# Magnitude products in pieces of 1280 and 1600 for VectorE or GpSimd; argument casts all on VectorE

## The chip, the cores and the metric

The kernel runs on one core of one Trainium2 chip. The metric is the time of one execution on the device in microseconds (us), less is better. A core has five engines with their own instruction queues: TensorE (PE, matrix products; PEld is its weight load), VectorE (DVE), ScalarE (ACT), GpSimd (POOL) and SyncE (SP, which here only issues transfers). ScalarE and GpSimd queues can issue transfers too. Each queue is worked off in order; engines wait for each other by semaphores.

## The reference

With `x` of 2048 positions and 640 channels, the result is `g * a + (1 - g) * b`:

```python
g = sigmoid((x * gate_w).sum(-1))                       # a gate for each position
# a: a state space model, as a long convolution along the positions
P = exp((dt * A)[:, :, None] * l)                       # 640 channels, 128 states, l = 0..2047
K = einsum('dn,dnl,dn->dl', C, P, dt * B).real          # one filter of 2048 taps for each channel
a = irfft(rfft(x padded) * rfft(K padded))[:2048] + x * Dskip
# b: a gated MLP that mixes positions
z = gelu(x @ w_in);  z1, z2 = halves of z;  z2 = layernorm(z2)
b = (z1 * (w_sp @ z2 + b_sp)) @ w_out
```

`A`, `B` and `C` are complex, so each tap is a sum of terms "magnitude times sine or cosine": `exp(dt * Re(A) * l)` is the magnitude, and `dt * Im(A) * l` plus a phase is the argument of the sine.

## The kernel before

**The filter.** A position is split as `l = (rough part) + (fine part)`, and the filter comes out of small matrix products of two tables for each channel, with the 128 states on the partitions. The 640 channels are cut into eight chunks of 80 (`SD = 80`). For chunk `c`, `k_tables(c)` fills a tile `ET` with:

- `E1`: two halves (sine `E1s` and cosine `E1`) of `NA = 20` rows of 80, 1600 elements each;
- `E2` and `M2`: 33 rows each, the sine and the cosine of the other factor, of which rows 1 to 16 (`ps_`) and 17 to 32 (`ns_`) are 1280 elements each. The negative rows of `E2` are first copied with a changed sign.

There are two `ET` tiles, used in turn (`z = c % 2`), so chunk `c + 2` may write its tile only when chunk `c` has been read.

The steps of a chunk are:

1. `si`: the arguments, `th` times 8, 16, ... (an int32 tile of 8 rows of 80; the low 16 bits are the angle). VectorE does it as one product with a constant (L896); GpSimd did it as eight instructions, one a row (L258). There are two such tiles a chunk.
2. `ci`: the same plus a quarter turn (16384), for the cosine (L258).
3. `eights`: the arguments `ai` of `E1`, on VectorE (L856, L863), and their quarter-turn copies `ci2` (L258). Tiles `ia` (three) and `ib` (two) are rings.
4. ScalarE takes the sine of each tile (L312) and writes it to `ET`.
5. The products with the magnitudes `mr` (tables of exponentials): L912 on `E2`, L913 and L914 on the two halves of `M2`, L923 on both halves of `E1` at once. All were VectorE's.
6. TensorE's `ps_k` (`k_sub`, L940 and L941): 320 small matrix products for a chunk, which read the whole of `ET`.

The exponentials for four chunks at a time come from `k_exps` on ScalarE, ahead of chunks 0 and 4; they overwrite the `mr` that the four chunks before read.

**What surrounds it.** `ps_k` is evicted to `kf` and stored; after chunk 5 the first 480 channels are read back in another layout (`k_expand`, the `xk` loads), go through a first stage (`conv_s1`, L1029), and the second stage (`conv_s2`) multiplies with the transformed input: `ps_u` (L1076), `ps_s2k` (L1083), the product on VectorE (L1085), `ps_v` (L1091). Its twiddle tables T and G (`tg_build`) are built only when all eight `ps_k` are done, since they take the memory of the tables. The last stage is `conv_i2` (`ps_i`, L1157 and L1159, evictions L1107, L1124, L1126).

The MLP's work fills TensorE in between: `z2_tile` at the start (L486), `z1_tile` in groups (L518, with the groups 2 and 3 tied to the phases after chunks 1 and 5), and eight `sp_block`s (L704 and L706 for `ps_g`, evicted as `vT` by VectorE at L710 and L713; then L727 for `ps_o`). The forward transform of the input is `s1_u` (L545, L549).

**What sets the order.** No queue is written by hand. Every step is a task with a list of engines that may do it and a cost in us for each, what it reads and writes, and a bias. `Plan.run` goes through time with these costs and gives each engine, when it is free, the ready task of the highest priority; the tables' bias lets them go ahead of the MLP. The order found is then emitted, fixed, for all engines and for the transfers. So a change of a cost, or of the engines that a task may use, re-sorts every queue.

```python
    AE = ("DVE", "POOL")
    A1 = ("DVE",)
    dv2 = lambda n: 0.15 + n / 1920.0
```

Of the kernel before, what the change touches and what calls it, by code (L numbers as in the profile page):

```python
# [10 lines left out]
ALU = mybir.AluOpType  # L11
# [9 lines left out]
NA = len(ATAB)  # L21
# [15 lines left out]
class Plan:  # L37
# [15 lines left out]
    def add(self, eng, cost, fn, r=(), w=(), hold_=(), fset=None, nbytes=0, hold=0.0, bias=0.0, deps=(), lag=()):  # L53
        i = len(self.tasks)
        d = set(deps)
        d.update(j for j, _ in lag)
        hs = set(hold_)
        for k in r:
            if isinstance(k, tuple) and isinstance(k[0], Handle):
                hs.add(k[0])  # L60
            elif isinstance(k, Handle):
                hs.add(k)
            d.update(self.lastw.get(k, ()))
            self.readers.setdefault(k, []).append(i)
        for k in w:
            if isinstance(k, tuple) and isinstance(k[0], Handle):
                hs.add(k[0])
            elif isinstance(k, Handle):
                hs.add(k)
            d.update(self.lastw.get(k, ()))  # L70
            d.update(self.readers.get(k, ()))
            self.lastw[k] = [i]
            self.readers[k] = []
        d.discard(i)
        engs = (eng,) if isinstance(eng, str) else tuple(eng)
        costs = (cost,) if isinstance(cost, (int, float)) else tuple(cost)
        self.tasks.append(dict(i=i, engs=engs, costs=costs, fn=fn, deps=d, hs=hs, fset=fset, nb=nbytes, hold=hold, bias=bias, res=hold_, lag=dict(lag)))
        return i
# [139 lines left out]
def kernel(  # L218
# [20 lines left out]
    P = 128  # L239
# [11 lines left out]
    SD = 80  # L251
    DRAM = bass.MemoryType.DRAM
    PSUM = bass.MemoryType.PSUM
    vec, act, pool, pe, sp = nc.vector, nc.scalar, nc.gpsimd, nc.tensor, nc.sync

    def ts_(eng, out_, in_, s1, s2, op0, op1=None):
        if op1 is None:
            eng.tensor_scalar(out=out_, in0=in_, scalar1=s1, scalar2=None, op0=op0)  # L258
        else:
            eng.tensor_scalar(out=out_, in0=in_, scalar1=s1, scalar2=s2, op0=op0, op1=op1)  # L260
# [26 lines left out]
    add, ring = pl.add, pl.ring  # L287
    E_ = {"PE": pe, "DVE": vec, "ACT": act, "POOL": pool, "SP": sp}
# [4 lines left out]
    dv2 = lambda n: 0.15 + n / 1920.0  # L293
# [16 lines left out]
    def actf(cost, out_, in_, func, r, w, scale=1.0, bias=0.0, deps=(), lag=()):  # L310
        fs = {ACT.Exp: "exp", ACT.Tanh: "gelu", ACT.Ln: "exp", ACT.Sin: "sin", ACT.Arctan: "sin", ACT.Gelu_apprx_tanh: "gelu"}.get(func)
        return add("ACT", cost, lambda e: act.activation(out=out_(), in_=in_(), func=func, scale=scale), r=r, w=w, fset=fs, bias=bias, deps=deps, lag=lag)  # L312
# [54 lines left out]
    for g in range(4):  # L367
        S_(dma("SP", lambda g=g: xT[:, :, 512 * g:512 * g + 512], lambda g=g: x2[512 * g:512 * g + 512, :], 700000, w=[("xT", g)], tr=True,
              bias=7000 - g if g < 2 else 6800 - 10 * g))
# [72 lines left out]
    for q in range(4):  # L442
        add("DVE", 0.2, lambda e, q=q: ts_(vec, F1[:, q // 2, q % 2, :], f1b[:].rearrange("p c k -> p (c k)"), mqs[:, q:q + 1], None, ALU.mult),
            r=["pre"], w=[("F1", q)], bias=9000)
# [14 lines left out]
    th = parm.tile([P, D], F32, name="th")  # L459
# [99 lines left out]
    for g in range(4):  # L559
# [10 lines left out]
        for st in range(4 * g, 4 * g + 4):  # L570
            add(("ACT", "DVE"), (1.1, 0.5), lambda e, st=st: ts_(vec, z2n[:, st, :], z2n[:, st, :], mv[:, st, 0:1], rstd[:, st:st + 1], ALU.subtract, ALU.mult) if e == "DVE" else
                act.activation(out=z2n[:, st, :], in_=z2n[:, st, :], func=ACT.Identity, scale=rstd[:, st:st + 1], bias=nmr[:, st:st + 1]),
                r=[("nmr", g), ("rstd", g), ("z2", st)], w=[("z2n", st)], bias=8000)
# [54 lines left out]
    for o, a in (("ax", "Wr"), ("at", "Wi")):  # L628
        add("DVE", dv1(D), lambda e, o=o, a=a: vec.scalar_tensor_tensor(out=ap_(o), in0=ap_(a), scalar=-1.0, in1=ap_(a), op0=ALU.mult, op1=ALU.max),
            r=[a], w=[o], bias=2500)  # L630
# [9 lines left out]
    def pstt(o, a, s1, b, op0, op1):  # L640
        add("DVE", dv1(D), lambda e: vec.scalar_tensor_tensor(out=ap_(o), in0=ap_(a), scalar=s1, in1=ap_(b), op0=op0, op1=op1), r=[a, b, "ptmp"], w=[o], bias=2500)
# [24 lines left out]
    for ab in range(2):  # L666
        for q in range(2):
            add("DVE", 0.2, lambda e, ab=ab, q=q: vec.tensor_copy(out=f1p[:, ab, :].rearrange("p (c q k) -> p q c k", q=2, c=2)[:, q], in_=F1[:, ab, q, :].rearrange("p (c k) -> p c k", c=2)),
                r=F1r, w=[("f1p", ab, q)], bias=900)
# [149 lines left out]
    AE = ("DVE", "POOL")  # L819
    A1 = ("DVE",)  # L820
# [4 lines left out]
    def RI(tag, name, dt):  # L825
        return sbt(KGP, tag, name, shB, dt, bufs={"ia": 3, "ib": 2}[tag])
# [55 lines left out]
    def k_tables(c):  # L882
        B0 = KB0 - 50 * c
        z, zm = c % 2, c % 4
        sl = lambda t: t[:, SD * c:SD * c + SD]
        mr = lambda a, b: X["mr"][:, zm, a:b, :]
        E1, E2, M2 = (lambda: X["E1", z]), (lambda: X["E2", z]), (lambda: X["M2", z])
        add(("DVE", "ACT", "POOL"), (0.2, 0.27, 1.0), lambda e: act.copy(out=M2()[:, 0:1, :], in_=mr(0, 1)) if e == "ACT" else E_[e].tensor_copy(out=M2()[:, 0:1, :], in_=mr(0, 1)), r=[("mr", 0, zm)], w=[("M2z", z)], bias=B0)
        ids = []
        for g in range(2):  # L890
            si = RI("ia", "si", I32)
            ci = RI("ib", "ci", I32)

            def mk_si(e, si=si, g=g):
                if e == "DVE":
                    return vec.tensor_tensor(out=si()[:], in0=sl(th).unsqueeze(1).to_broadcast(shB), in1=cB[:, GB2 * g:GB2 * g + GB2].unsqueeze(2).to_broadcast(shB), op=ALU.mult)  # L896
                for j in range(GB2):
                    ts_(pool, row(si(), j), sl(th), 8.0 * (GB2 * g + j + 1), None, ALU.mult)
            add(AE, (0.95, 7.0), mk_si, r=["th", "kg"], w=[si], bias=B0)
            add(AE, (0.57, 2.6), lambda e, si=si, ci=ci: ts_(E_[e], ci()[:], si()[:], 16384.0, None, ALU.add), r=[si], w=[ci], bias=B0)  # L900
            gs = slice(GB2 * g + 1, GB2 * g + GB2 + 1)
            ids.append(actf(ac(GB2 * SD), lambda gs=gs: E2()[:, gs, :], lambda si=si: lo16(si()[:], shB), ACT.Sin, [si], [("E2p", z, g)], scale=SINS, bias=B0, deps=phase[0]))
            ids.append(actf(ac(GB2 * SD), lambda gs=gs: M2()[:, gs, :], lambda ci=ci: lo16(ci()[:], shB), ACT.Sin, [ci], [("M2p", z, g)], scale=SINS, bias=B0, deps=phase[0]))
        if c == 0:
            ids.append(add("ACT", 0.72, lambda e: act.activation(out=phi[:], in_=phi[:], func=ACT.Arctan), r=["phi"], w=["phi"], fset="sin", bias=B0 + 90, deps=phase[0]))
            pstt("phi", "phi", 8.0 * 65536.0 / (2.0 * PI), "al", ALU.mult, ALU.mult)
            ptt("phi", "phi", "be", ALU.add, ("DVE",))
        ep, mp = [("E2p", z, g) for g in range(2)], [("M2p", z, g) for g in range(2)]
        ps_, ns_ = slice(1, 17), slice(17, 33)
        mrp, mrn = [("mr", k, zm) for k in range(1, 17)], [("mr", k, zm) for k in range(17, 33)]  # L910
        add("DVE", dv4(16 * SD), lambda e: ts_(vec, E2()[:, ns_, :], E2()[:, ps_, :], -1.0, None, ALU.mult), r=ep, w=[("E2n", z)], bias=B0)
        add("DVE", dv2(32 * SD), lambda e: vec.tensor_tensor(out=E2()[:, 1:33, :], in0=E2()[:, 1:33, :], in1=mr(1, 33), op=ALU.mult), r=mrp + mrn + ep + [("E2n", z)], w=ep + [("E2n", z)], bias=B0)  # L912
        add("DVE", dv2(16 * SD), lambda e: vec.tensor_tensor(out=M2()[:, ns_, :], in0=M2()[:, ps_, :], in1=mr(17, 33), op=ALU.mult), r=mrn + mp, w=[("M2n", z)], bias=B0)  # L913
        add("DVE", dv2(16 * SD), lambda e: vec.tensor_tensor(out=M2()[:, ps_, :], in0=M2()[:, ps_, :], in1=mr(1, 17), op=ALU.mult), r=mrp + mp, w=mp, bias=B0)  # L914
        for gi, nr, ai in eights(lambda: sl(th), lambda: sl(phi), ["th", "phi", "kg"], B0):
            ci = RI("ib", "ci2", I32)
            sh = [P, nr, SD]
            add(AE, (dv2(nr * SD) + 0.09, 0.5 + nr * SD / 300), lambda e, ai=ai, ci=ci, nr=nr: ts_(E_[e], ci()[:, 0:nr, :], ai()[:, 0:nr, :], 16384.0, None, ALU.add), r=[(ai, j) for j in range(nr)], w=[ci], bias=B0)
            rs = slice(8 * gi, 8 * gi + nr)
            ids.append(actf(ac(nr * SD), lambda rs=rs: E1()[:, NA:2 * NA, :][:, rs, :], lambda ai=ai, nr=nr, sh=sh: lo16(ai()[:, 0:nr, :], sh), ACT.Sin, [(ai, j) for j in range(nr)], [("E1s", z, gi)], scale=-SINS, bias=B0, deps=phase[0]))  # L920
            ids.append(actf(ac(nr * SD), lambda rs=rs: E1()[:, 0:NA, :][:, rs, :], lambda ci=ci, nr=nr, sh=sh: lo16(ci()[:, 0:nr, :], sh), ACT.Sin, [ci], [("E1", z, gi)], scale=SINS, bias=B0, deps=phase[0]))
        ks = [(nm, z, q) for nm in ("E1", "E1s") for q in range(3)]
        add("DVE", dv2(2 * NA * SD), lambda e: vec.tensor_tensor(out=E1().rearrange("p (y a) d -> p y a d", y=2), in0=E1().rearrange("p (y a) d -> p y a d", y=2),  # L923
            in1=mr(33, 33 + NA).unsqueeze(1).to_broadcast([P, 2, NA, SD]), op=ALU.mult), r=[("mr", 33 + q, zm) for q in range(5)] + ks, w=ks, bias=B0)
        return ids

    SQ = 20
# [316 lines left out]
```

## Time and profile before

| | us |
|---|---|
| median of 3 runs | 402.55 (399.67 to 402.74) |
| the profiled execution | 403.62 |
| its span in the profile | 401.8 |
| TensorE busy | 330.6 (82% of the span) |
| VectorE busy | 280.2 (70%) |
| ScalarE busy | 240.2 (60%) |
| GpSimd busy | 155.8 (39%) |
| TensorE clock granted, mean | 0.939 of full speed |

A row of the groups has the line and the engine, the operation, what it writes and reads, the shape and the count; behind the first bar the busy time in us and the mean of one in ns; behind the second the idle time of the engine just before these instructions, with who ended it. A row of a timeline has the start in us, the time it took, the engine and the instruction; several alike in a row are merged ("x4" takes four), and the bracket tells how long the engine had been idle before, and for what. The slices cut the span into 40 parts; each digit is the busy share of an engine in tenths.

### The profile page before, as it was taken

To read this page: it belongs to the slowest core of one execution; us is meant where nothing else is said; L and a number is where in the kernel's file an instruction comes from. 1 tells how busy PE (TensorE), PEld (TensorE's weight loads), DVE (VectorE), ACT (ScalarE), POOL (GpSimd) and SP (SyncE) were. 2 spreads that over 40 slices of the span, in tenths; PEclk is the share of its full clock that TensorE was granted. 3 is DMA by queue.
4 is the path that set the end of the run, shared out by engine and by line. 5 is a ranking of instruction groups with operands and counts; after the bars stand their busy time and mean duration, and the time that the engine had idled before them with its cause. 6 is when DMAs were issued, how large, how long until landed. Compare 5 with 4: busy or idle time off the path is not lost. (4 is left out here: it accounts for less than half of the span.)

```text
span 401.8 us, 8388 instructions
## 1 busy us (share of the span) xinstructions
PE 330.6 (82%) x3218; PEld 213.9 (53%) x3225; DVE 280.2 (70%) x516; ACT 240.2 (60%) x425; POOL 155.8 (39%) x172
## 2 busy tenths in 40 slices
PE   0699589999999999999999955999978678863571
PEld 0255235667777667787776833776723233452220
DVE  4099981378988839784677757677588577999852
ACT  4187373299995667579924473555458657752240
POOL 3048840230077419672295639425475000000212
PEclk9999789999999999999999995999989989997586
DMA  7897729969883579393507249475435398530145
GB/s 174 161 168 116 164 63 183 295 152 239 192 207 100 131 174 255 106 184 44 139 0 124 69 67 229 131 239 124 146 105 172 98 298 285 150 89 2 33 137 165
DMA packets 111449, 59.37 MB, mean 148 GB/s; under 512 B 80262, under 2 KB 108050, under 8 KB 111410
## 3 DMA queue, kind: packets, MB, share of 16 engines
q1 hardware_dynamic: 109698, 55.02, 57.3%
q0 software_dynamic: 1712, 3.82, 3.5%
q8 instruction: 25, 0.41, 0.5%
q14 instruction: 14, 0.11, 0.1%
HBM read 24.73 MB, written 19.47 MB: 110 GB/s over the span
## 5 line engine op out<-in xcount | busy, mean ns | idle before, releaser
L704 PE MATMUL ps_g<-wT,z2n 128*128 128x256 bf16 (+1 forms) x896 | 113.3, 276 | 9.7 <-DVE vT L710 9.4
L704 PEld LDWEIGHTS <-z2n 128*128 128x128 bf16 (+1 forms) x896 | 87.3, 102 | 28.1 <-issue 9.8
L258 POOL TENSOR_SCALAR ci<-ai 128x640 int32<-128x640 int32 x11 | 29.3, 2673 | 65.9 <-ACT ET L312 41.1
L1085 DVE TENSOR_TENSOR p<-ps_s2k,us 128x960 bf16<-128x960 f32 (+1 forms) x48 | 47.9, 1038 | 8.5 <-PE ps_s2k L1083 6.6
L258 POOL TENSOR_SCALAR si<-th 128x80 int32<-128x80 f32 x64 | 43.7, 683 | 23.2 <-DVE t3p L653 18.1
L486 PE MATMUL ps_z<-Win,xT 128*128 128x432 bf16 (+1 forms) x160 | 35.2, 387 | 12.3 <-DMA xT<-in_A_u_dram 6.5
L1091 PE MATMUL ps_v<-p,G 128*128 128x480 bf16 (+1 forms) x128 | 26.2, 310 | 14.7 <-DVE p L1085 10.0
L1093 ACT CAST vs<-ps_v 128x480 bf16<-128x480 f32 (+1 forms) x48 | 24.7, 516 | 20.1 <-PE ps_v L1091 19.9
L312 ACT ACTIVATE ET<-ci 128x640 bf16<-128x640 int16 (+1 forms) x40 | 26.5, 676 | 13.2 <-DVE ci L258 9.2
L727 PE MATMUL ps_o<-Wout,vT 128*128 128x320 bf16 (+1 forms) x224 | 33.0, 299 | 0.0
L486 PEld LDWEIGHTS <-xT 128*128 128x128 bf16 x160 | 17.1, 107 | 29.9 <-issue 12.3
L518 PE MATMUL ps_z<-xg,Win 128*128 128x512 bf16 (+1 forms) x133 | 31.2, 379 | 0.6 <-ACT zt L312 0.2
L940 PE MATMUL ps_k<-ET 128*32 128x33 bf16 x640 | 27.7, 259 | 0.7 <-DVE ET L923 0.7
L319 ACT CAST us<-ps_u 128x480 bf16<-128x480 f32 (+1 forms) x48 | 24.7, 518 | 5.6 <-PE ps_u L1076 3.8
L940 PEld LDWEIGHTS <-ET 128*32 128x32 bf16 x640 | 26.8, 193 | 2.2 <-DVE ET L923 0.9
L1126 POOL TENSOR_TENSOR obr<-tm,obr 128x160 bf16<-128x160 bf16 (+1 forms) x8 | 4.9, 634 | 59.3 <-ACT tm L1124 53.5
L941 PE MATMUL ps_k<-ET 128*32 128x33 bf16 x640 | 27.6, 258 | 0.0
L1083 PE MATMUL ps_s2k<-fk,T 128*128 128x480 bf16 (+1 forms) x128 | 25.5, 312 | 2.0 <-DVE p L1085 1.6
L941 PEld LDWEIGHTS <-ET 128*32 128x32 bf16 x640 | 27.1, 195 | 0.0
L727 PEld LDWEIGHTS <-vT 128*128 128x128 bf16 (+1 forms) x224 | 21.5, 97 | 9.1
L490 ACT ACTIVATE z2n<-ps_z 128x864 bf16<-128x864 f32 x16 | 14.2, 885 | 19.9 <-PE ps_z L486 19.9
L1091 PEld LDWEIGHTS <-G 128*128 128x128 bf16 x128 | 10.2, 100 | 28.5 <-DVE p L1085 13.9
(188 smaller groups left out, 622.0 us busy)
## 6 DMA issues: line engine op xcount, KB each, us to landing
FU_d<-s1u SPq DMA_DIRECT2D x16, 240.0 KB
fu<-FU_d SPq DMA_DIRECT2D x16, 240.0 KB
fk<-FK_d SPq DMA_DIRECT2D x16, 240.0 KB
z_d<-zt SPq DMA_DIRECT2D x24, 128.0 KB
z1t<-z_d SPq DMA_DIRECT2D x8, 384.0 KB
xf<-in_A_u_dram SPq DMA_DIRECT2D x8, 320.0 KB
FK_d<-s1k POOLq DMA_DIRECT2D x5, 480.0 KB, 3.9
Win<-in_B_w_in_dram SPq DMA_DIRECT2D x2, 1080.0 KB
```

Of the source, the lines that this page charges most:

```text
L258: eng.tensor_scalar(out=out_, in0=in_, scalar1=s1, scalar2=None, op0=op0)
L312: return add("ACT", cost, lambda e: act.activation(out=out_(), in_=in_(), func=func, scale=scale), r=r, w=w, fset=fs, bias=bias, deps=deps ...
L319: (vec.tensor_copy if e == "DVE" else act.copy)(out=out_(), in_=in_())
L486: pe.matmul(ps()[:, h, 0:432 + h], lhsT=xT[:, i, 128 * st:128 * st + 128], rhs=Win2[:, i, 432 * h:432 * h + 432 + h], start=(i == 0), stop ...
L518: pe.matmul(ps()[0:fs, ft - f0, :], lhsT=Win1[:, i, 128 * ft:128 * ft + fs], rhs=xg()[:, i, :], start=(i == 0), stop=(i == ND - 1))
L704: pe.matmul(ps()[0:fs, ft - f0, :], lhsT=z2n[:, st, 128 * ft:128 * ft + fs], rhs=wT()[:, st, :], start=(st == 0), stop=False)
L727: pe.matmul(ps()[:], lhsT=vT[ft // 2]()[0:fs, ft % 2, 128 * r:128 * r + 128], rhs=Wout[0:fs, ft, HD * h:HD * h + HD], start=(ft == 0), sto ...
L940: pe.matmul(o_, lhsT=ET[:, 0:32, d], rhs=M2[:, :, d], start=True, stop=False, tile_position=(0, 32 * q))
L941: pe.matmul(o_, lhsT=ET[:, NA:NA + 32, d], rhs=E2[:, :, d], start=False, stop=True, tile_position=(0, 32 * q))
L1083: pe.matmul(ps()[:, i, W * n:W * n + W], lhsT=TK(k + n, i), rhs=fk()[:, j + n, :], start=True, stop=True)
L1085: add("DVE", dv1(2 * NW), lambda e, p12=p12, ps=ps, us=us: vec.tensor_tensor(out=p12()[:, :, 0:NW], in0=ps()[:, :, 0:NW], in1=us()[:, 0:NW ...
L1091: pe.matmul(pv()[:, W * n:W * n + W], lhsT=GV(k + n, i), rhs=p12()[:, i, W * n:W * n + W], start=(i == 0), stop=(i == 1))
```

## The change

- `si` and `ci` of `k_tables` may be done by VectorE alone; so may `ci2`. (GpSimd's eight-row form of `si` stays in the code, unused.)
- The product of 2560 elements on `E2` becomes two of 1280, one for the positive rows and one for the negative; the product of 3200 on `E1` becomes two of 1600, for `E1s` and `E1`. The two on `M2` keep their size.
- All six products of a chunk, 48 in all, may be done by VectorE or by GpSimd. The cost given for GpSimd is `0.45 + n / 700`, for VectorE `0.15 + n / 1920`.

```diff
-            add(AE, (0.95, 7.0), mk_si, r=["th", "kg"], w=[si], bias=B0)
-            add(AE, (0.57, 2.6), lambda e, si=si, ci=ci: ts_(E_[e], ci()[:], si()[:], 16384.0, None, ALU.add), r=[si], w=[ci], bias=B0)
+            add(A1, (0.95,), mk_si, r=["th", "kg"], w=[si], bias=B0)
+            add(A1, (0.57,), lambda e, si=si, ci=ci: ts_(E_[e], ci()[:], si()[:], 16384.0, None, ALU.add), r=[si], w=[ci], bias=B0)
...
-        add("DVE", dv2(32 * SD), lambda e: vec.tensor_tensor(out=E2()[:, 1:33, :], in0=E2()[:, 1:33, :], in1=mr(1, 33), op=ALU.mult), r=mrp + mrn + ep + [("E2n", z)], w=ep + [("E2n", z)], bias=B0)
-        add("DVE", dv2(16 * SD), lambda e: vec.tensor_tensor(out=M2()[:, ns_, :], in0=M2()[:, ps_, :], in1=mr(17, 33), op=ALU.mult), r=mrn + mp, w=[("M2n", z)], bias=B0)
-        add("DVE", dv2(16 * SD), lambda e: vec.tensor_tensor(out=M2()[:, ps_, :], in0=M2()[:, ps_, :], in1=mr(1, 17), op=ALU.mult), r=mrp + mp, w=mp, bias=B0)
+        PM = lambda n: (dv2(n), 0.45 + n / 700)
+        add(AE, PM(16 * SD), lambda e: E_[e].tensor_tensor(out=M2()[:, ns_, :], in0=M2()[:, ps_, :], in1=mr(17, 33), op=ALU.mult), r=mrn + mp, w=[("M2n", z)], bias=B0)
+        add(AE, PM(16 * SD), lambda e: E_[e].tensor_tensor(out=M2()[:, ps_, :], in0=M2()[:, ps_, :], in1=mr(1, 17), op=ALU.mult), r=mrp + mp, w=mp, bias=B0)
+        add(AE, PM(16 * SD), lambda e: E_[e].tensor_tensor(out=E2()[:, ps_, :], in0=E2()[:, ps_, :], in1=mr(1, 17), op=ALU.mult), r=mrp + ep + [("E2n", z)], w=ep, bias=B0)
+        add(AE, PM(16 * SD), lambda e: E_[e].tensor_tensor(out=E2()[:, ns_, :], in0=E2()[:, ns_, :], in1=mr(17, 33), op=ALU.mult), r=mrn + [("E2n", z)], w=[("E2n", z)], bias=B0)
...
-            add(AE, (dv2(nr * SD) + 0.09, 0.5 + nr * SD / 300), lambda e, ai=ai, ci=ci, nr=nr: ts_(E_[e], ci()[:, 0:nr, :], ai()[:, 0:nr, :], 16384.0, None, ALU.add), r=[(ai, j) for j in range(nr)], w=[ci], bias=B0)
+            add(A1, (dv2(nr * SD) + 0.09,), lambda e, ai=ai, ci=ci, nr=nr: ts_(E_[e], ci()[:, 0:nr, :], ai()[:, 0:nr, :], 16384.0, None, ALU.add), r=[(ai, j) for j in range(nr)], w=[ci], bias=B0)
...
-        ks = [(nm, z, q) for nm in ("E1", "E1s") for q in range(3)]
-        add("DVE", dv2(2 * NA * SD), lambda e: vec.tensor_tensor(out=E1().rearrange("p (y a) d -> p y a d", y=2), in0=E1().rearrange("p (y a) d -> p y a d", y=2),
-            in1=mr(33, 33 + NA).unsqueeze(1).to_broadcast([P, 2, NA, SD]), op=ALU.mult), r=[("mr", 33 + q, zm) for q in range(5)] + ks, w=ks, bias=B0)
+        for y, nm in enumerate(("E1s", "E1")):
+            ks = [(nm, z, q) for q in range(3)]
+            rs = slice(NA - NA * y, 2 * NA - NA * y)
+            add(AE, PM(NA * SD), lambda e, rs=rs: E_[e].tensor_tensor(out=E1()[:, rs, :], in0=E1()[:, rs, :], in1=mr(33, 33 + NA), op=ALU.mult), r=[("mr", 33 + q, zm) for q in range(5)] + ks, w=ks, bias=B0)
```

## The prediction

> **What bounds the kernel now.** I read the page's busy shares and slices first, to find the stage that the change touches.
>
> ```profile
> PE 330.6 (82%) x3218; PEld 213.9 (53%) x3225; DVE 280.2 (70%) x516; ACT 240.2 (60%) x425; POOL 155.8 (39%) x172
> ...
> PE   0699589999999999999999955999978678863571
> DVE  4099981378988839784677757677588577999852
> POOL 3048840230077419672295639425475000000212
> ```
>
> A slice is 10 us. From 60 to 270 us TensorE is busy nine tenths or more, but for slices 23 and 24; the change lies in 110 to 270, where the tables of the eight chunks are built. TensorE works there through a fixed order in which each chunk's `ps_k` (L940, L941) is placed just when its tables are due. The timelines of VectorE and TensorE:
>
> ```profile
> 119.75 1.83 DVE L923 TENSOR_TENSOR ET<-ET,mr 128x3200 bf16<-128x3200 bf16 x1 [1.15 <-ACT ET L312]
> ...
> 121.87 0.30 PE L940 MATMUL ps_k<-ET 128*32 128x33 bf16 x4
> ...
> 138.05 0.30 PE L940 MATMUL ps_k<-ET 128*32 128x33 bf16 x4 [0.72 <-DVE ET L923]
> ```
>
> Chunk 0's last product ends at 121.58 and its `ps_k` starts at 121.87; chunk 1 waits 0.72 us for it. A table later than planned is a stall. The one large stall:
>
> ```profile
> 243.31 0.83 DVE L896 TENSOR_TENSOR si<-th,cB 128x640 int32<-128x640 f32 x1 [1.70 <-POOL ci L258]
> ...
> 245.02 1.28 DVE L710 TENSOR_TENSOR vT<-ps_g,z1t 128x512 bf16<-128x512 f32 x2
> ...
> 245.76 3.57 PE L704 MATMUL ps_g<-wT,z2n 128*128 128x256 bf16 x16 [9.15 <-DVE vT L710]
> ```
>
> TensorE waits 9.15 us for an eviction that stands on VectorE behind an `si` that waits for GpSimd's cast. `ps_k` starts at 121.9, 138.1, 158.7, 176.8, 209.9, 227.5, 250.5 and 269.1; `ps_v`, the first output of the convolution's second stage, at 295.4, after which VectorE leads to the end (78.7 of 107 us busy). The groups by shape give the prices:
>
> ```profile
> L258 POOL TENSOR_SCALAR si<-th 128x80 int32<-128x80 f32 x64 | 43.7, 683 | 23.2 <-DVE t3p L653 18.1 <-ACT s1u L319 1.1
> L258 POOL TENSOR_SCALAR ci<-ai 128x640 int32<-128x640 int32 x11 | 29.3, 2673 | 65.9 <-ACT ET L312 41.1 <-DVE ai L863 23.9 <-ACT s1u L319 1.0
> L258 POOL TENSOR_SCALAR ci<-si 128x640 int32<-128x640 int32 x6 | 12.8, 2126 | 0.8 <-ACT ET L312 0.5
> L1126 POOL TENSOR_TENSOR obr<-tm,obr 128x160 bf16<-128x160 bf16 x6 | 2.8, 484 | 53.6 <-ACT tm L1124 53.5
> L1126 POOL TENSOR_TENSOR obr<-tm,obr 128x480 bf16<-128x480 bf16 x2 | 2.1, 1088 | 5.7 <-DMA obr<-ob_d 5.7
> L923 DVE TENSOR_TENSOR ET<-ET,mr 128x3200 bf16<-128x3200 bf16 x8 | 14.6, 1825 | 1.4 <-ACT ET L312 1.4
> L912 DVE TENSOR_TENSOR ET<-ET,mr 128x2560 bf16<-128x2560 bf16 x8 | 12.1, 1507 | 0.0
> L914 DVE TENSOR_TENSOR ET<-ET,mr 128x1280 bf16<-128x1280 bf16 x8 | 6.6, 828 | 0.0
> ```
>
> The number ahead of the second bar is the mean of one in ns. GpSimd's products exist only in two small shapes, in the tail.
>
> How a GpSimd product sits beside VectorE shows early in the timeline:
>
> ```profile
> 20.54 1.68 DVE L258 TENSOR_SCALAR mv<-zs 128x2 f32<-128x2 f32 x1 [0.57 <-ACT z2n L490]
> 20.77 1.41 POOL L600 TENSOR_TENSOR t<-nat_Cim,nat_Bim 128x640 f32<-128x640 bf16 x1
> ...
> 23.09 1.54 POOL L600 TENSOR_TENSOR Wr<-Wr,t 128x640 f32<-128x640 f32 x1 [0.91 <-DVE zs L565]
> 23.13 1.52 DVE L566 SCALAR_TENSOR_TENSOR mv<-zs 128x2 f32<-128x2 f32 x1
> ```
>
> Two-element VectorE instructions whose fellows take 0.15 us last until GpSimd's product ends.
>
> **What the Trainium skill says.** "SBUF — State Buffer", section "Who interferes with whom": VectorE's second port pair is GpSimd's only one; an instruction of VectorE with two SBUF inputs, or in a two-port mode, and a GpSimd instruction that reads SBUF exclude each other, whole instructions at a time. The trace agrees, with 1.5 and 1.4 us lost above. "GPSIMD Engine Reference", section 3.1: about 2.6 cycles an element at 1.2 GHz for two inputs, an estimate of 2.8 us for 1280; the trace's slope is smaller, (1088 − 484)/320 = 1.89 ns an element. "VectorE: DVE Perf Modes", the perf-mode tier table: bf16 products run two elements a cycle; the trace agrees (2560 in 1.507 us).
>
> **The change part by part.** By the queues of the changed kernel GpSimd takes 19 of the 32 products of 1280 and 7 of the 16 of 1600; VectorE keeps 13 and 9.
>
> *Products.* VectorE loses L912, L913, L914, L923: 12.1 + 6.6 + 6.6 + 14.6 = 39.9 us. It keeps 13 × 0.82 + 9 × 1.00 (between 828 for 1280 and 1507 for 2560) = 19.7. GpSimd: 1088 + 800 × 1.89 ns = 2.60 us for 1280 and 3.20 for 1600, so 19 × 2.60 + 7 × 3.20 = 71.8 us. Bounds: 2.28 and 2.74, the planner's own price (`PM`), from below; above, the stretch that GpSimd's casts show beside VectorE: `si` alone takes 0.416 us (median), `ci` 1.81, so 64 × 0.416 + 17 × 1.81 = 57.4 us became 85.8, 1.49 times.
>
> *Casts and arguments.* GpSimd loses these 85.8 us. VectorE gains 8 `si` at 0.825 = 6.6 (before.py's 64 pieces were 8 of them) and 17 `ci` at 0.505 = 8.6. Net: VectorE −5.0 us, GpSimd −14.0. Neither is worth that in time: both are sums over engines that are not full. What matters is that `si` was work ahead of need, and a product is the last step ahead of `ps_k`. No DMA is added or dropped, but the planner re-sorts the queues: GpSimd's stores of `kf` and its ten `xk` loads (0.55 us each) now stand between products of chunks 5, 6 and 7. The stall at 236 to 245 loses its cause.
>
> *The hold.* GpSimd's two-input work from 20.8 to 47 us (L600 7.1 us, L615 4.2) took from VectorE 1.5 + 1.35 + 0.45 + 0.54 + 0.64 + 1.4 = 5.9 us, read as each slow instruction less its fellows: 52%. At 71.8/8 = 9.0 us of products a chunk that is 4.7 us of VectorE's time a chunk. Queued behind a held instruction are the arguments of E1, the casts ScalarE's sines read, and `vT`, whose lateness stops TensorE. Bounds: nothing, if the holds fall into VectorE's idle time (VectorE is busy 90.2 of 128 us from 122 to 250), and all 4.7. I take a third, 1.6, plus the underpricing, 2 × 0.32 + 0.46 = 1.1: 2.7 us a chunk.
>
> *The order of TensorE.* I summed both orders at rates from the timeline's starts (L704 and L706 0.118 us each, L518 0.232, L727 0.137, L545 0.20, a `ps_k` 3.35). Between one `ps_k` and the next the old order holds 15.3, 20.6, 17.7, 31.8, 17.7, 11.4, 18.1; the trace has 16.2, 20.7, 18.0, 33.1, 17.6, 23.1, 18.6, so all but the 23.1 run without a stall. The new order holds 11.3, 19.1, 18.9, 19.5, 17.1, 14.6, 15.8, with 5.0 more before the first and 31.7 instead of 22.7 from the last `ps_k` to `ps_v`. It asks for tables sooner.
>
> The fourth gap can't be 19.5: from 174.9 ScalarE spends 19.8 us on exponentials, which overwrite what chunk 3's products read, then 1.3 on a table load and some 6.1 on sines, and then come the products, some 3.5: 31.
>
> *The sum.* First `ps_k` 121.9 + 5.0 + 2.7 = 129.6. Six gaps 96.8 + 6 × 2.7 = 113.0; the fourth 31; last `ps_k` 273.6. Plus 31.7: `ps_v` at 305.3, 9.9 later. The rest (106.4 us) I leave as it is: TensorE's order there is 2.3 us longer, beside VectorE. The profiled execution took 403.62 (span 401.8), the median is 1.07 less: 413.5 profiled, **412.5** as a median.
>
> **The rivals.** *Holds in idle time*: only the underpricing stays. 128.0, gaps 96.8 + 6.6 + 31, `ps_v` at 294.1: 401.3. For it speaks VectorE's idle share; against it, that VectorE is an in-order queue on the tables' path. *The shorter order comes true*: in addition chunk 3's products end early enough that the exponentials start ahead of `ps_k`, a fourth gap of 24: `ps_v` at 287.1, 8.3 earlier, 394. It decides where the last `ps_k` starts before 263.7 (295.4 − 31.7). For it speaks the old stall of 9.15 us that GpSimd's cast caused; against it, a product three times as long on GpSimd at the end of the chain. *Two thirds of the hold on the path*: 4.3 a chunk, `ps_v` at 316.5, 424. That the change does nothing is excluded: 26 products are in GpSimd's queue.
>
> **How the numbers follow.** One per cent, about what can be told from no change, is 4 us. Forecast (407 to 419) 0.54, the heavy hold 0.16, holds in idle time 0.17, the shorter order 0.13: slower 0.70, same 0.17, faster 0.13. The range of 396 to 425 leaves out most of the fastest case and the end of the slowest.
>
> **What would show it.** Right: GpSimd's 1280 products at 2.6 us or more; VectorE's short L856 and casts at several times their 0.2 and 0.5 us beside them; TensorE waiting at L940 for POOL; the last `ps_k` near 274. Wrong: VectorE's means unchanged, GpSimd's products near 2.3, or the fourth gap well below 31 with the last `ps_k` before 264.

## The result, and the profile after

The changed kernel takes 430.41 us (median of 4 runs, 428.94 to 433.97), the kernel before beside it 402.28: a ratio of 1.073, 95% interval 1.0645 to 1.081. It is slower by 28 us, where the forecast was 10 slower and the range ended at 425. The profiled execution took 433.97 us (span 432.1), before 403.62 (401.8). The page's busy shares and slices (a slice is now 10.8 us):

```profile
PE 342.6 (79%) x3220; PEld 218.5 (51%) x3225; DVE 323.8 (75%) x528; ACT 239.2 (55%) x424; POOL 156.6 (36%) x124
...
PE   0799599999777999578898998698999858865471
DVE  3189940898987949989469998984549767899852
POOL 2157810000743605581225829655267030000111
PEclk9999699999968969796888999899999999998586
```

VectorE was to lose 5 us of work and 37.6 us to the hold (4.7 in each of eight chunks), and is busy 43.6 us longer; TensorE does the same work in 12 us more. TensorE's row of nines, which before ran from slice 6 to slice 28 but for 23 and 24, is broken from slice 10 (108 us) on. How it starts, in the timelines of the three engines for chunk 0 (start, time taken, engine, instruction; in the bracket the idle time before and its releaser):

```profile
109.49 2.61 POOL L915 TENSOR_TENSOR ET<-ET,mr 128x1280 bf16<-128x1280 bf16 x1 [23.82 <-DVE ET L258]
109.78 2.99 DVE L600 TENSOR_TENSOR phi<-phi,be 128x640 f32<-128x640 f32 x1
113.44 5.80 DVE L856 SCALAR_TENSOR_TENSOR ai<-th,phi 128x80 int32<-128x80 f32 x6
113.59 2.69 POOL L914 TENSOR_TENSOR ET<-ET,mr 128x1280 bf16<-128x1280 bf16 x1 [1.50 <-DVE ET L913]
116.24 2.60 POOL L916 TENSOR_TENSOR ET<-ET,mr 128x1280 bf16<-128x1280 bf16 x1
120.34 0.54 DVE L258 TENSOR_SCALAR ob<-ps_o,omg 128x320 bf16<-128x320 f32 x1
120.94 2.03 PE L727 MATMUL ps_o<-Wout,vT 128*128 128x320 bf16 x7 [5.13 <-DVE ob L258]
122.76 5.21 PE L704 MATMUL ps_g<-wT,z2n 128*128 128x256 bf16 x28
128.36 3.22 POOL L927 TENSOR_TENSOR ET<-ET,mr 128x1600 bf16<-128x1600 bf16 x1 [0.76 <-ACT ET L312]
128.43 3.24 DVE L856 SCALAR_TENSOR_TENSOR ai<-th,phi 128x80 int32<-128x80 f32 x1
132.32 2.33 PE L704 MATMUL ps_g<-wT,z2n 128*128 128x256 bf16 x16 [3.39 <-DVE vT L710]
```

Six adds of 80 elements (L856) last 5.80 us, from 113.44 on, while GpSimd's two products run from 113.59 to 118.84; one add lasts 3.24 us, as long as the product of 1600 that began 0.07 us before it. Behind the six adds stands the eviction `ob` (L258). It takes its usual 0.54 us, but TensorE has waited 5.13 us for it, and its next 28 matmuls of L704 take 5.21 us. The groups by shape (busy time, mean ns of one):

```profile
L927 POOL TENSOR_TENSOR ET<-ET,mr 128x1600 bf16<-128x1600 bf16 x7 | 26.2, 3747 | 12.5 <-ACT ET L312 12.5
L856 DVE SCALAR_TENSOR_TENSOR ai<-th,phi 128x80 int32<-128x80 f32 x64 | 25.8, 447 | 2.0 <-ACT ET L312 2.0
L863 DVE SCALAR_TENSOR_TENSOR ai<-th,ai 128x160 int32<-128x160 f32 x16 | 14.3, 895 | 0.0
L258 DVE TENSOR_SCALAR ci<-ai 128x320 int32<-128x320 int32 x8 | 12.8, 1599 | 0.7 <-ACT ET L312 0.7
L914 POOL TENSOR_TENSOR ET<-ET,mr 128x1280 bf16<-128x1280 bf16 x4 | 10.5, 2620 | 1.7 <-DVE ET L913 1.5
L914 DVE TENSOR_TENSOR ET<-ET,mr 128x1280 bf16<-128x1280 bf16 x4 | 11.0, 2738 | 0.0
```

GpSimd's 1280 products take 2.6 to 2.8 us on the mean and its 26 products 78.2 us in all, near the 71.8 forecast. It is VectorE's rows that are off: an add 447 ns (279 before), the 160-wide one 895 (321), the 320-wide cast 1599 (345). The four L914 products that VectorE kept take 2.74 us each where GpSimd needs 2.62.

The eight `ps_k` start at 138.9, 151.0, 179.1, 207.3, 236.1, 253.4, 271.3 and 290.8, `ps_v` at 326.6; after that come 105.5 us (106.4 before). So all of the loss lies ahead of `ps_v`. TensorE's waits for evictions and tables (total us, times, longest):

```profile
PE ps_g L704 <- DVE vT L710: 8.3, 5, 3.4
PE ps_o L727 <- DVE ob L258: 5.8, 2, 5.1
PE ps_s1x L549 <- ACT s1u L319: 4.3, 1, 4.3
PE ps_k L943 <- DVE ET L927: 3.0, 2, 2.8
PE ps_k L943 <- POOL ET L927: 1.9, 1, 1.9
```

It waits more for VectorE's evictions (14.1 us) than for tables (6.5 with the 1.6 at L944); the 4.3 us are one wait for an eviction of ScalarE. All but the first line are new or grew. The wait for `vT` was 9.4 us before, nearly all of it the one stall of 9.2, which is gone; the five now are others.

### The profile page after: what moved, and what is told of

It reads as the page before. It is cut to its first block, busy times and chain, and to the rows that moved or that the text cites. A ratio compares the mean times of both kernels' runs of the same rounds, so it can differ in the third digit from the quotient of the medians.

```text
span 432.1 us, 8357 instructions
## 1 busy us (share of the span) xinstructions
PE 342.6 (79%) x3220; PEld 218.5 (51%) x3225; DVE 323.8 (75%) x528; ACT 239.2 (55%) x424; POOL 156.6 (36%) x124
## 5 line engine op out<-in xcount | busy, mean ns | idle before, releaser
L704 PE MATMUL ps_g<-wT,z2n 128*128 128x256 bf16 (+1 forms) x896 | 119.6, 285 | 9.7 <-DVE vT L710 8.3
L704 PEld LDWEIGHTS <-z2n 128*128 128x128 bf16 (+1 forms) x896 | 89.5, 105 | 37.1 <-issue 15.7
L727 PE MATMUL ps_o<-Wout,vT 128*128 128x320 bf16 (+1 forms) x224 | 38.4, 331 | 7.5 <-DVE ob L258 5.8
L312 ACT ACTIVATE ET<-ci 128x640 bf16<-128x640 int16 (+1 forms) x40 | 25.8, 678 | 25.5 <-DVE ci L258 25.5
L727 PEld LDWEIGHTS <-vT 128*128 128x128 bf16 (+1 forms) x224 | 23.7, 106 | 21.6 <-issue 10.2
L1094 PE MATMUL ps_v<-p,G 128*128 128x480 bf16 (+1 forms) x128 | 25.6, 306 | 10.8 <-DVE p L1088 9.5
L518 PE MATMUL ps_z<-xg,Win 128*128 128x512 bf16 (+1 forms) x135 | 32.6, 389 | 1.2 <-ACT zt L312 0.8
L913 POOL TENSOR_TENSOR ET<-ET,mr 128x1280 bf16<-128x1280 bf16 x7 | 19.4, 2765 | 32.0 <-ACT ET L312 24.7
L927 POOL TENSOR_TENSOR ET<-ET,mr 128x1600 bf16<-128x1600 bf16 x7 | 26.2, 3747 | 12.5 <-ACT ET L312 12.5
L944 PE MATMUL ps_k<-ET 128*32 128x33 bf16 x640 | 27.9, 258 | 2.1 <-DVE ET L916 1.6
L944 PEld LDWEIGHTS <-ET 128*32 128x32 bf16 x640 | 27.4, 195 | 0.0
L888 POOL COPY ET<-mr 128x80 bf16<-128x80 bf16 x6 | 4.9, 817 | 61.9 <-PE ps_k L944 32.7
L856 DVE SCALAR_TENSOR_TENSOR ai<-th,phi 128x80 int32<-128x80 f32 x64 | 25.8, 447 | 2.0 <-ACT ET L312 2.0
L1086 PE MATMUL ps_s2k<-fk,T 128*128 128x480 bf16 (+1 forms) x128 | 24.5, 299 | 1.2 <-DVE p L1088 0.7
```

The lines of the kernel that those rows point to most:

```text
L518: pe.matmul(ps()[0:fs, ft - f0, :], lhsT=Win1[:, i, 128 * ft:128 * ft + fs], rhs=xg()[:, i, :], start=(i == 0), stop=(i == ND - 1))
L704: pe.matmul(ps()[0:fs, ft - f0, :], lhsT=z2n[:, st, 128 * ft:128 * ft + fs], rhs=wT()[:, st, :], start=(st == 0), stop=False)
L727: pe.matmul(ps()[:], lhsT=vT[ft // 2]()[0:fs, ft % 2, 128 * r:128 * r + 128], rhs=Wout[0:fs, ft, HD * h:HD * h + HD], start=(ft == 0), sto ...
L856: add("DVE", 0.12 + dv1(SD), lambda e, j=j, r_=r_, t=t: vec.scalar_tensor_tensor(out=row(t(), j), in0=src(), scalar=float(ATAB[r_]), in1=a ...
L927: add(AE, PM(NA * SD), lambda e, rs=rs: E_[e].tensor_tensor(out=E1()[:, rs, :], in0=E1()[:, rs, :], in1=mr(33, 33 + NA), op=ALU.mult), r=[ ...
L944: pe.matmul(o_, lhsT=ET[:, NA:NA + 32, d], rhs=E2[:, :, d], start=False, stop=True, tile_position=(0, 32 * q))
```

## The experiments

The theories. A: GpSimd's product holds VectorE, whole instructions at a time; what queues behind the held ones, evictions and arguments, makes TensorE late. B: the delay alone: tables come late, since the planner prices GpSimd too low and the last steps ahead of `ps_k` take three times as long. C: the casts moved to VectorE, or the split, cost the time. D: the lower clock of TensorE is a cause of its own.

### The same plan, all products issued by VectorE

```diff
-add(AE, PM(16 * SD), lambda e: E_[e].tensor_tensor(...))
+add(AE, PM(16 * SD), lambda e: vec.tensor_tensor(...))
```

The same edit on all six products. The plan is made with the old prices and engines, so every queue but VectorE's and GpSimd's keeps its order.

> The plan and the order of every queue stay those of the changed kernel, but the 26 products that stood in GpSimd's queue are issued by VectorE. Theory A (GpSimd's two-input products hold VectorE): VectorE loses some 48.6 us of hold and gains 19 x 0.82 + 7 x 1.00 = 22.6 us of products, so its busy time falls from 323.8 to about 298, the mean of the argument adds (L856) from 447 to below 300 ns, and the time from 430 to 400-412. Theory B (the leaner order of TensorE and the moved casts cost the time, whichever engine multiplies): the time stays at 420-432. Theory D (TensorE's clock fell by itself): 420-430 with the granted clock in the table stage still near 0.86.

It took 400.7 us (median of 4 runs, 395.1 to 402.2). The ratio on record, 0.985 of before (0.977 to 0.993), rests on two of the four and is unclear. As it would have been a gain, it was run again:

> The same kernel as in the first set of runs (the changed kernel's plan, all products issued by VectorE), with more rounds, since it stood below the kernel before. Theory A with the order of TensorE worth what the sum said (8.3 us less up to ps_v where tables are in time): 395-400. If the first reading was chance: 400-404.

Here 400.27 us (22 runs), 0.9954 (0.993 to 0.998): half a per cent under before. It is the base for what follows. The groups, waits and `ps_k` stretch of this second profile:

```profile
L856 DVE SCALAR_TENSOR_TENSOR ai<-th,phi 128x80 int32<-128x80 f32 x64 | 12.1, 232 | 1.9 <-ACT ET L312 1.9
L863 DVE SCALAR_TENSOR_TENSOR ai<-th,ai 128x160 int32<-128x160 f32 x16 | 5.1, 317 | 0.0
L258 DVE TENSOR_SCALAR ci<-ai 128x320 int32<-128x320 int32 x8 | 2.5, 318 | 1.1 <-ACT ET L312 1.1
L914 DVE TENSOR_TENSOR ET<-ET,mr 128x1280 bf16<-128x1280 bf16 x8 | 6.5, 816 | 0.0
```
```profile
PE ps_g L704 <- DVE vT L710: 1.8, 5, 0.5
PE ps_o L727 <- DVE ob L258: 1.0, 2, 0.6
```

Every mean is back (add 232 ns, cast 318), and `ps_k` waits for nothing. VectorE is busy 286.3 us; without the 26 products (19 of 0.816 and 7 of 0.98, 22.4 us) that is 263.9, against 323.8 in the changed kernel: **59.9 us of hold**, 77% of the 78.2 us that GpSimd's products took. The clock, in the windows from 110 us to `ps_v` (columns: busy time of TensorE, its weight loads, VectorE, ScalarE and GpSimd, each with its count; granted clock; DMA share; GB/s), first of the changed kernel and then of this one:

```profile
110.00:326.63 216.63, 185.51 (x2301) 131.80 (x2303) 172.42 (x265) 113.56 (x182) 109.05 (x65) 0.90 0.48 115
```
```profile
110.00:293.09 183.09, 172.80 (x2317) 127.43 (x2320) 136.78 (x295) 116.36 (x186) 37.73 (x39) 0.99 0.60 138
```

With the products off GpSimd the clock is at 0.99 by itself, so D falls as a cause of its own. Of the 33.5 us between the two, 12.7 is TensorE's own work at a lower clock and 20.8 is idle. (At 110 us the changed kernel stood some 2.6 us further in the same order, so what its tables lost is a little more.) That the clock falls after stalls is what the Trainium skill says ("TensorE: Matmul & The Clock Gate", Part 1: the array is throttled unless it is busy); the trace agrees in the 28 matmuls of L704, 3.22 us in this kernel and 5.21 soon after the stall of 5.13. The leaner order of TensorE (this expectation's B) and C's casts are in this kernel too and cost nothing. The kernel takes hold and delay away together; further runs below part them.

### The products on VectorE with a plan made for it; the split alone; the products alone

```diff
-PM = lambda n: (dv2(n), 0.45 + n / 700)
-add(AE, PM(...), ...)
+PM1 = lambda n: (dv2(n),)
+add(A1, PM1(...), ...)
```

> The split products and the casts all on VectorE, and the plan made for that. Theory A: no hold is left, VectorE is busy 280.2 + 15.2 (casts) + about 2 (more and shorter products) = 297 us, and the time is 398-408. Theory C (the casts on VectorE or the split itself cost the time): 412-430, with VectorE late ahead of the ps_k of the tables.

406.12 us, 1.010 (1.0065 to 1.013): within the expectation of A, and about 1% over before.

The split alone has this edit, and takes `si`, `ci` and `ci2` back to `AE` with their old prices:

> Only the split: six products a chunk, all on VectorE, the casts and arguments for VectorE or GpSimd as before. Theory A: no new hold, two more fixed costs of VectorE a chunk (48 x 0.82 or so against 39.9 us in all, under 3 us): within 1.5% of before, 397-408. Theory C' (the split itself costs): over 410.

400.98 us, 0.9957 (0.993 to 0.998): the split costs nothing. The products alone keep the changed kernel's products and take the casts back to `AE`:

> Only the products are changed: split, for VectorE or GpSimd (this plan gives GpSimd 15 of 1280 and 1 of 1600, 42.2 us); the casts and arguments may go to GpSimd as before. Theory A: slow, by the hold of 42.2 us of products, 33.7 x 42.2 / 71.8 = 20 us over what the plan gives without: 412-425. Theory C (the loss comes from the casts on VectorE): within 1% of before, 398-407.

424.6 us, 1.055 (1.050 to 1.060), with the casts where they were before. A's 20 us are 23.6 over the split alone. C falls on both sides: the casts without products on GpSimd cost at most 1%, the products without the casts over 5%.

### The true price in the plan

```diff
-PM = lambda n: (dv2(n), 0.45 + n / 700)
+PM = lambda n: (dv2(n), 0.17 + n / 528)
```

> The changed kernel with GpSimd's price in the plan raised to what the trace measured (0.17 + n/528: 2.59 us for 1280, 3.20 for 1600, instead of 2.28 and 2.74). Theory B (the plan places ps_k too early since the price is too low): 405-415. Theory A: the holds remain as far as products remain on GpSimd; with 20 or more products there the time is 418-432.

441.6 us, 1.096 (1.090 to 1.1025), outside both expectations, and slower than A had it. The plan still gives GpSimd 25 products (19 of 1280, 6 of 1600) and VectorE is busy 329.0 us. B's part that speaks of the price falls; why this plan loses 11 us more than the changed kernel's isn't settled. The price that is missing is on the other engine: no figure for GpSimd's own time tells the planner that VectorE stands meanwhile.

### One input instead of two

```diff
+for s in (in0, out):
+    pool.tensor_scalar(out=out, in0=s, scalar1=1.0, scalar2=0.0, op0=ALU.mult, op1=ALU.add)
```

in place of each `tensor_tensor` of GpSimd.

> Each product in GpSimd's queue is replaced by two in-place multiply-by-one-and-add-zero instructions with one SBUF input, on the same tiles and in the same place in every queue. It leaves out those multiplications by the magnitudes. Theory A in its narrow form (the second input is what holds VectorE): VectorE's means go back (L856 below 320 ns, the 320-wide cast to about 0.35 us) and the time falls to 400-414, if the pair on GpSimd takes no longer than the 2.6 or 3.2 us of the product. Theory A in its broad form (any GpSimd instruction on SBUF holds VectorE): 420-435. Theory B (tables late because GpSimd's step is the last of the chain, with no hold needed): 420-432 with VectorE's means gone back.

422.99 us, 1.049 (1.043 to 1.055). The pair takes 3.06 us for 1280 instead of 2.6, and VectorE, busy 313.0 us, loses 49.1 of the pairs' 84.0 us, 58%. Its means don't go back as B had it: an add takes 338 ns, the 320-wide cast 968. So A holds in its broad form: that GpSimd reads SBUF with one input is enough to hold VectorE. Not all of the loss need be hold here, since the pair also comes later: TensorE waits 5.3 us for GpSimd at `ps_k`.

### The bench: who holds whom

A kernel of its own: five streams of VectorE, each alone and beside four streams of GpSimd that start with it.

```diff
+vec.tensor_copy(out=sv[:, 0:1], in_=sg[:, 1:2])
+pool.tensor_copy(out=sg[:, 0:1], in_=sv[:, 0:1])
+for _ in range(gc): gf(tg)
+for _ in range(cnt): vf(tv)
```

> A bench alone: it leaves the whole computation out and writes zeros. Five streams of VectorE (30 argument adds of 80 with two inputs from SBUF, 16 int32 casts of 640, 9 bf16 products of 1280, 12 products of 512 with one input from PSUM, 16 scalings of 320 from PSUM), each of 6 to 8 us, run once alone and once beside each of four GpSimd streams started at the same moment: 3 products of 1280 with two inputs, 5 one-input steps of 1280, 4 int32 casts of 640, 8 iotas that only write. Theory A (whole instructions exclude each other): beside the products, the adds, the casts and VectorE's own products take their own time plus the 7.8 us of GpSimd's (mean of an add 0.24 to 0.49 us, of a cast 0.49 to 0.97), the streams from PSUM keep their means, and GpSimd's products stay at 2.6 us. Rival (the two share bandwidth in turn): both sides stretch, GpSimd's products to 4 us or more, and VectorE's means rise by a half at most. The iotas: no change on VectorE if only reads collide.

The groups by shape, where the name gives the stream and its neighbour (`Vadd_Gprod`: adds of VectorE beside products of GpSimd):

```profile
L50 DVE SCALAR_TENSOR_TENSOR Vadd_Gnone<-f,f 128x80 int32<-128x80 f32 x30 | 7.3, 242 | 1.0
L50 DVE SCALAR_TENSOR_TENSOR Vadd_Gprod<-f,f 128x80 int32<-128x80 f32 x30 | 14.3, 478 | 1.0
L50 DVE SCALAR_TENSOR_TENSOR Vadd_Gone<-f,f 128x80 int32<-128x80 f32 x30 | 12.4, 414 | 1.0
L50 DVE SCALAR_TENSOR_TENSOR Vadd_Giota<-f,f 128x80 int32<-128x80 f32 x30 | 7.3, 242 | 1.0
L51 DVE TENSOR_SCALAR Vcast_Gnone<-i 128x640 int32<-128x640 int32 x16 | 7.9, 493 | 0.5
L51 DVE TENSOR_SCALAR Vcast_Gprod<-i 128x640 int32<-128x640 int32 x16 | 14.9, 929 | 0.5
L51 DVE TENSOR_SCALAR Vcast_Giota<-i 128x640 int32<-128x640 int32 x16 | 11.1, 692 | 0.5
L53 DVE TENSOR_TENSOR Vevic_Gnone<-p,b 128x512 bf16<-128x512 f32 x12 | 8.3, 690 | 0.4
L53 DVE TENSOR_TENSOR Vevic_Gprod<-p,b 128x512 bf16<-128x512 f32 x12 | 8.3, 690 | 0.4
L58 POOL TENSOR_TENSOR gprod_vadd<-gb,gm 128x1280 bf16<-128x1280 bf16 x3 | 7.8, 2597 | 0.2
```

Three products of GpSimd, 7.8 us, cost VectorE's adds 7.0 us and its casts 7.0: nine tenths of GpSimd's time, with VectorE at work all the while. VectorE's own products went from 824 to 1599 ns (7.0 us again). GpSimd's products stay at 2597 ns beside the adds (2681 beside the casts, 2903 beside VectorE's own products), where sharing in turn was to make them 4 us or more; so the two don't share. The evictions that read PSUM lose nothing. This is the rule of the Trainium skill's page "SBUF — State Buffer", section "Who interferes with whom", and the runs agree with it in each case, also that a GpSimd instruction that only writes leaves adds of two inputs alone (242 ns beside iotas) but not a cast, which by that page can run in a two-port mode (493 to 692).

### Hold without GpSimd in the tables, and delay without most of the hold

```diff
+vec.tensor_tensor(out=out, in0=in0, in1=in1, op=op)
+if e == "POOL" and zm:
+    s = X["mr"][:, zm - 1, 0:out.shape[1], :]
+    pool.tensor_copy(out=s[:, 0, 0:1], in_=out[:, 0, 0:1])
+    pool.tensor_tensor(out=s, in0=s, in1=s, op=ALU.mult)
```

> The hold without the delay: every product is issued by VectorE in its place, and where the plan had given it to GpSimd, GpSimd then multiplies as large a piece of the magnitudes of the chunk before, which nothing reads any more, so no table waits for it. This is done in six of the eight chunks (1, 2, 3, 5, 6, 7), 13 of 1280 and 5 of 1600, 49.8 us of GpSimd's products against 71.8. Theory A: the hold alone makes the loss, 400.3 + 30.1 x 49.8 / 71.8 = 421, in 413-424, VectorE busy some 286 + 0.75 x 49.8 = 323. Theory B (delay): 400-407. If both share it: 406-413.

421.25 us, 1.0515 (1.045 to 1.058). No table takes a product from GpSimd here, and 18 products whose result nothing reads (idle products, from here on), instead of the 26, cost 21.0 us over the base of 400.3, where A had said 421. The timeline of chunk 2 in it:

```profile
154.59 2.32 POOL L918 TENSOR_TENSOR mr<-mr 128x1280 bf16<-128x1280 bf16 x1
154.62 3.87 DVE L914 TENSOR_TENSOR ET<-ET,mr 128x1280 bf16<-128x1280 bf16 x2
159.15 4.37 DVE L914 TENSOR_TENSOR ET<-ET,mr 128x1600 bf16<-128x1600 bf16 x2
159.35 3.49 POOL L918 TENSOR_TENSOR mr<-mr 128x1600 bf16<-128x1600 bf16 x1
163.44 1.27 DVE L710 TENSOR_TENSOR vT<-ps_g,z1t 128x512 bf16<-128x512 f32 x2
164.17 1.01 PE L704 MATMUL ps_g<-wT,z2n 128*128 128x256 bf16 x4 [7.48 <-DVE vT L710]
```

Two products of VectorE take 3.87 us instead of 1.64, two more 4.37 instead of 1.96; the eviction `vT` behind them isn't held itself, but TensorE waits 7.48 us for it. No table from GpSimd is in that wait.

Not all of the 21.0 us is hold, though, against what was expected: two waits do pass through GpSimd.

```profile
ACT mr L312 <- POOL mr L918: 6.6, 2, 4.7
PE ps_s1k L1038 <- DMA xk<-KA_d: 5.6, 1, 5.6
```

The exponentials of chunks 4 to 7 overwrite the magnitudes that an idle product still writes, so ScalarE waits 6.6 us; through it VectorE, and behind it an eviction that TensorE needs, come 1 us later. And ten `xk` loads stand in GpSimd's queue behind an idle product: they go out from 259.6 us, 8 us after chunk 6's `ps_k`, in the base 1 us ahead of it; TensorE waits 5.6 us for them. Less these the hold alone comes to 21.0 − 5.6 − 1.0 = 14.4 us, an estimate, and with 400.3 + 14.4 = 414.7 still in A's range (413 to 424). What ScalarE's wait cost beyond the 1 us isn't shown.

The counterpart replaces GpSimd's products by steps that only write:

```diff
+pool.tensor_copy(out=out[:, 0, 0:1], in_=in0[:, 0, 0:1])
+for _ in range(4):
+    pool.iota(out.rearrange("p a d -> p (a d)").bitcast(F32), pattern=[[1, 40 * out.shape[1]]], ...)
```

> The delay without most of the hold: the changed kernel's plan, with each of GpSimd's 26 products replaced by a copy of one element and four iotas that only write (0.3 + 4 x 0.66 = 2.96 us for 1280 and some 3.6 for 1600, from the bench), on the same tiles at the same places. It leaves out those products, and the tables hold numbers of no meaning. In the bench iotas left VectorE's adds and products alone (0.242 and 0.824 us) and cost only its casts (0.49 to 0.69). Theory A (the hold makes the loss): 401-410, VectorE busy under 295. Theory B (the loss is that tables come late, since GpSimd's step is the long one ahead of ps_k): 416-432.

411.21 us, 1.028 (1.021 to 1.035), between the two expectations and just over A's end. The copy took 0.63 us on the mean, so a step takes some 3.5 us for 1280 and 4.0 for 1600, longer than the product it stands for. TensorE waits 14.4 us for GpSimd at `ps_k`, against 1.9 in the changed kernel; VectorE, busy 274.4, still loses 10.5 us. So delay costs something, 10.9 us at the most in this kernel, though the delay is larger here than in the changed kernel.

### Which products

The plan of the changed kernel, with one kind of the products issued by VectorE: in the first the pieces of 1600, in the second those of 1280.

```diff
-add(AE, PM(NA * SD), lambda e, rs=rs: E_[e].tensor_tensor(...))
+add(AE, PM(NA * SD), lambda e, rs=rs: vec.tensor_tensor(...))
```

> The changed kernel's plan, with the 19 products of 1280 still on GpSimd and the 7 of 1600 (E1, the last step ahead of ps_k) issued by VectorE in the same places. With none on GpSimd the same plan stood at 0.985 of before (396.6), with all at 430. Theory A (each microsecond of GpSimd's products costs alike through the hold): 19 x 2.60 = 49.4 of 71.8 us remain, so 396.6 + 33.7 x 0.69 = 419.8, in 415-424. Theory B (what costs is that the last step ahead of ps_k takes 3.2 us on GpSimd instead of 1.0 on VectorE): most of the loss goes, 397-408.

> The other half: the 7 products of 1600 on GpSimd, the 19 of 1280 issued by VectorE in their places. Theory A: 22.4 of 71.8 us remain, 396.6 + 33.7 x 0.31 = 407, in 402-412. Theory B: 418-430.

423.4 us (1.051, 1.045 to 1.057) and 418.37 us (1.038, 1.033 to 1.043). The first is in A's range. The second isn't: it lies in B's, at its lower end, 6 us above A's. Both of A's figures were reckoned from a base of 396.6; from 400.3 they would be 421 and 410. In the trace of the second TensorE waits 8.8 us for `vT` and 1.5 us for GpSimd at `ps_k`. All that stood on GpSimd, over the base of 400.3 (the runs come from several chips, on which the kernel before took 400.9 to 402.7, so a cost is good to 1 or 2 us; VectorE's loss is its busy time, less 286.3, plus its own time for the products it was spared):

| GpSimd does | GpSimd's time for it, us | VectorE loses, us | cost, us |
|---|---|---|---|
| all 26 products (the changed kernel) | 78.2 | 59.9 | 30.1 |
| 19 of 1280 | 51.7 | 41.8 | 23.1 |
| 7 of 1600 | 26.6 | 13.1 | 18.1 |
| 26 pairs of one input | 84.0 | 49.1 | 22.7 |
| 18 idle products, in no table | 51.1 | 31.2 | 21.0 |
| 26 steps that only write, after a copy of one element | 94.0 | 10.5 | 10.9 |

The halves add up to 41.2, not 30.1, so the costs aren't additive; that a stall which one product makes covers part of the next one's would fit, but isn't shown. The seven of 1600 cost more for the VectorE time they take than any other row. They stand last ahead of `ps_k`, so delay and hold come together there; how much of the 18.1 is which stays open.

## Why the prediction failed

The direction and the mechanism held; the size didn't. Step by step:

- **Products.** GpSimd's took 2.59 to 3.18 us (1280) and mostly 3.2 to 3.3 (1600), near the slope's 2.60 and 3.20; one took 3.78 and one 6.28. Right but for these: 78.2 us in all against 71.8.
- **Casts and arguments, net VectorE −5.0 us.** The base with everything on VectorE is busy 286.3, and the changed kernel's own work 263.9 against 280.2 before: −16.3, where the holds by GpSimd's casts are gone too (an add took 279 ns before and takes 232 in the base). For VectorE as a whole the prediction comes to 280.2 − 5.0 + 37.6 = 312.8 us, only 11.0 under the measured 323.8: the 11.3 that it missed here hid half of the 22.3 that it missed in the hold.
- **The hold, the step that failed.** Two terms of it were too small. The first is the share of GpSimd's time that VectorE loses. 52% was read from L600 and L615 between 20.8 and 47 us; here it was 77%, 59.9 us, 7.5 us a chunk and not 4.7, and the bench gives 90%. VectorE was no less busy in that early stretch (25.4 of 26.2 us), but in part with other work: its BATCH_NORM_STATS2 (L498, 16 of them from 25.5 us on), for one, take 0.585 to 0.612 us each, beside GpSimd's products too, so they aren't held. The adds, casts and products of the tables are. The second term is "I take a third", the part of the hold on the path. The prediction counted VectorE as idle for 38 of 128 us, but in the timeline of chunk 0 the adds and casts stand ready just when GpSimd's products run. Between the changed kernel and the same plan without GpSimd's products `ps_v` moves 33.5 us, where 18.9 were summed, with the underpricing. These two terms make 14.6 us of the miss. The 33.5 are 56% of the hold, but they contain the delay too; with the 18 idle products `ps_v` moves 19.4 us for 31.2 of hold, and some 12.8 (41%) without the two waits through GpSimd. How much of the 33.5 is the hold's own stays open.
- **Underpricing, 1.1 a chunk.** The true price didn't help (441.6), and no run shows the term by itself.
- **The order of TensorE.** In the base, with no product on GpSimd, the first `ps_k` starts at 129.1 (the sum without hold: 126.9) and the gaps are 10.9, 20.4, 19.6, 23.7, 17.1, 15.0, 20.9 with 36.4 to `ps_v`; the sum had 11.3, 19.1, 18.9, 31, 17.1, 14.6, 15.8 and 31.7. The fourth gap was not bound at 31. Its chain of exponentials, sines and products does take 31.7 us in the base (172.1 to 203.8), but it starts 8.0 us ahead of chunk 3's `ps_k` and not 1.9, as before; there the rival with 24 was right. The last two were 5.1 and 4.7 longer. The last stretch had run 3.6 us over its sum before too (26.3 against 22.7), and the prediction, which compared only the gaps, didn't carry that over. In all `ps_v` comes at 293.1, not at the sum's 286.4 without hold and underpricing, so this adds 6.7 us.
- **The sum.** `ps_v` at 326.6 instead of 305.3: 14.6 + 6.7. After it 105.5 us, as said (106.4). These are the profiled executions; by the medians the miss is 430.41 − 412.5 = 17.9 us, since the one profiled is the slowest of the changed kernel's four.

What the sum lacked altogether is TensorE's clock: 12.7 of the 33.5 us are its own work, slower after stalls (a part of the 14.6 above, not beside them). With the 18 idle products the loss was there with only 3.4 us of it (176.2 us busy from 110 us to `ps_v`, against 172.8), so it adds to the loss but isn't needed for it.

The rival with two thirds on the path took 4.3 us a chunk, and the runs give 33.5/8 = 4.2, the delay included. That is luck in part: it took two thirds of a hold that was too small, and the underpricing. It ended at 424 because it used the same order sum and no hold in the fourth gap (28.8 against 23.7 in the base). Of the signs named for being right three were seen: GpSimd's products at 2.6 us, VectorE's adds and casts stretched beside them, and TensorE waiting for GpSimd at `ps_k`, once, for 1.9 us. The fourth wasn't: the last `ps_k` starts at 290.8, not near 274. The sign that mattered most, TensorE waiting for evictions, wasn't named: the prediction named `vT` as queued behind held work and then looked for the loss at `ps_k`.

## What to carry to other kernels

Work given to GpSimd that reads SBUF isn't beside VectorE's work but in its place, where VectorE does what was held here: two inputs from SBUF, or the casts. Charge VectorE with most of its duration (77% in this kernel, 90% in the bench), unless VectorE is at that time idle or evicting PSUM (690 ns with and without), and then ask what stands behind the held instruction in VectorE's queue. A short eviction there can cost TensorE the whole hold (it waited 5.1 and 7.5 us here) and some clock besides. A planner that prices each engine by itself can't see this, and a better price for GpSimd alone didn't mend it.

## What was not expected

- The hold goes both ways. One product of 1600 on GpSimd took 6.28 us beside four VectorE instructions back to back, and chunk 2's `ps_k` waited its 1.9 us for that product; in the kernel with iotas a copy of a single element took 4.28 us while VectorE ran three products and two `si` without a gap. In these cases it is the engine that comes second that stands.
- Both engines stretched when GpSimd's iotas ran beside VectorE's casts (664 to 823 ns, 493 to 692).
- Twenty-six moved products made 28 us of loss while GpSimd was busy for hardly longer than before (156.6 us against 155.8). Its busy time says nothing of what it takes from VectorE: before, its casts took 85.8 us, and the add's mean beside them was 279 ns.
